# A delta-rule and Mish kernel on one core: sign by Prelu, one join for two, low bits on GpSimd, and a new work order

## The chip, the cores and the metric

The kernel runs on one core of one Trainium2 chip. The metric is the device time of one execution in microseconds (us); lower is better. The core has five instruction queues that are spoken of here: TensorE (PE in the profile; PEld is its weight load), VectorE (DVE), ScalarE (ACT), GpSimd (POOL) and SyncE (SP, which here only issues transfers). Each queue is carried out in the order in which it is written: an instruction that waits holds up everything behind it on its engine.

## What is computed

Two parts, the second fed by the first. A delta rule runs over 768 steps for 32 heads of 48 dimensions, and a feed-forward layer takes its output:

```python
k_n = k / (norm(k) + 1e-06)
for t in range(S):
    y[t] = q[t] @ state
    state = state + beta[t] * outer(k_n[t], v[t] - k_n[t] @ state)
x = y.transpose(0, 2, 1, 3).reshape(3072, 384)
h = x @ w_in
g = h * tanh(softplus(h))
out = g @ w_out
```

q, k, v and beta arrive as fp32. w_in (384 x 2048) and w_out (2048 x 384) arrive as fp64, and the core has to turn them into pairs of 32-bit numbers (a high part and what is left) before the layer can use them.

## The kernel before

**The delta rule.** Time is cut into 12 chunks n of 64 steps, taken in pairs g = n // 2. For a pair, `early` turns k round (L546), forms the products of the keys with each other on TensorE (`gram`), takes the norms' square roots (`norms`, `guess`, `root`) and solves a triangular system on VectorE, step by step (L688 and L689, two instructions a step). For g = 0 and 1 the system is solved in halves of 16, which `merge` joins with two sets of small products, `ma` and `mb`, and an addition on VectorE (L748). Then, for each chunk, TensorE's products `ta`, `tb` (stages `s_a2` and `s_b2`), `gq`, `pz` and `py`/`ps` (`s_gq`, `s_z`, `s_y`) give the chunk's output y and carry the state on; ScalarE and VectorE copy every result out of PSUM before the next product can use it.

**The layer.** `moe(n)` works on the 256 rows of one chunk: 8 times `up` (L1122, 18 products each, tile `h`), Mish on ScalarE (L1139, tile `e`), a high and a low part of the result (L1140 on ScalarE, L1141 on VectorE, tile `g`), and `down` (L1133, 12 products each, tile `acc`).

**The weights.** `convert(k)` turns one of 28 pieces of fp64 words (`parts`: 12 of w_in, tiles `ri`, 512 columns; 16 of w_out, tiles `ro`, 384 columns; four `o` behind every three `i`) into two fp32r tiles. The steps are: ScalarE scales the upper words by 2^-112 (L437); GpSimd clamps (L451) and writes sign times zero over the upper words (L448), VectorE doing the clamp of piece 6; VectorE joins twice (L455: once shifted left by 3 with the sign, once with the lower words shifted right by 29); ScalarE writes the high part (L467); the low part is a subtraction on VectorE (L478) for pieces 0 to 10, and for pieces 11 to 27 two products on TensorE (L472, L474) that ScalarE copies out (L476). `cvd` says which piece an `up` or a `down` needs: `up` 0 and 1 need pieces 0 to 2, `up` 2 and 3 pieces 7 to 9, and so on.

**The order.** No instruction is placed by hand. Every piece of work is an `op` with an engine, an estimated duration, a rank (`prio`), its predecessors and its buffers; `Plan.run` plays the program through with these estimates, always takes the ready piece of best rank, and so writes each engine's queue. It also estimates the transfers (`kb`, `line`, `flying`), and where it sees TensorE idle during the first part it puts in products on zeros (`fill`, L527, and `tiny`, L512), which keep TensorE busy and compute nothing. Its estimates set the order alone; on the chip every engine waits on semaphores for what it really needs. Transfers of weights go to SP in order; from piece 6 on, the load of piece k is issued only after L437 of piece k - 4 (`PACE`).

Of the kernel before, what the change touches and what calls it, by code (L numbers as in the profile page):

```python
# [10 lines left out]
I32 = mybir.dt.int32  # L11
BF16 = mybir.dt.bfloat16
# [56 lines left out]
class Plan:  # L69
# [48 lines left out]
    def run(self):  # L118
        there, due, group, cold = self.THERE, None, False, True
        free, line, used, ready, flying, chain = {}, 0.0, self.used, {}, [], {}  # L120
        for o in self.ops:
# [3 lines left out]
            free.setdefault(o.engine, 0.0)  # L125
# [9 lines left out]
        def when(o):  # L135
            late = 0.0 if o.engine != "PE" else 0.12 if o.prio < -50 else 0.12 + (self.MARGIN if o.prio < 1.9 else 0.1)
            t = max([a.free + (late if not a.kb or o.prio < -50 or o.prio > 1.5 else 2.5) if a.engine != o.engine or (a.kb and o.sync) else a.start + a.took
# [12 lines left out]
            if o.kb and len(flying) >= 8:  # L150
                t = max(t, flying[-8])
# [6 lines left out]
        while todo:  # L158
# [32 lines left out]
            if o.words and self.FILL_FROM < t < self.FILL_TO:  # L191
                us = self.SHARE * (t - free[e]) - 0.2
                n = self.fill(us) if us > self.FILL else 0
                if n:
                    _, there, due = self.feed(free[e], us, 4 * n, there, due, line)
            free[e] = t + o.took
            if o.words:
                _, there, due = self.feed(t, o.took, o.words, there, due, line)
            if o.kb:

                line = max(line, t + 1.6)
                line += o.kb
                o.free = line + 0.8
                flying.append(o.free)
            else:
                o.free = t + o.took + self.SEEN[e]
# [22 lines left out]
def kernel(  # L229
# [16 lines left out]
    P = 128  # L246
# [165 lines left out]
    def convert(k, got, loads):  # L412
# [23 lines left out]
        def scaled():  # L436
            marks[copied[k]] = nc.scalar.activation(a(), words()[:, :, 1].bitcast(F32), AF.Copy, scale=2.0 ** -112).ins  # L437
# [22 lines left out]
        e = "DVE" if k in SIGN_DVE else "POOL"  # L460
        o = op(e, 0.13 + 0.38 * u if e == "DVE" else 0.3 + 0.45 * u, prio, lambda: sign(e), o, bufs=held)
        o = op("DVE", 0.05 + 0.65 * u, prio, lambda: join(words()[:, :, 1], 3, ALU.logical_shift_left), o, bufs=held)
        o = op("DVE", 0.05 + 0.65 * u, prio, lambda: join(words()[:, :, 0], 29, ALU.logical_shift_right), o, bufs=held)
# [6 lines left out]
        if k in LO_PE:  # L470
# [3 lines left out]
            p2 = op("PE", 0.03 + 0.22 * u, prio, lambda: nc.tensor.matmul(  # L474
# [62 lines left out]
    def early(g, at, gate=None):  # L537
# [102 lines left out]

        def root():

            ss, y, rc, nb = (small[x] for x in ("ss", "y", "rc", "nb"))
# [3 lines left out]
            nc.vector.reciprocal(rc, ss)  # L647
            nc.vector.scalar_tensor_tensor(nb, rc, -1.0, rc, op0=ALU.mult, op1=ALU.mult)
# [8 lines left out]
        def scale():  # L657
            nb = small["nb"]
            nc.vector.tensor_tensor(out=nb, in0=nb, in1=betaT[:, g, :], op=ALU.mult)
# [643 lines left out]
```

## Time and profile before

| | us |
| --- | --- |
| median of 3 runs | 616.37 |
| lowest, highest run | 615.85, 617.23 |
| the profiled execution's own time | 618.65 |
| its span, first to last instruction | 616.9 |
| PE busy in the span | 595.7 (97%) |
| DVE busy | 433.4 (70%) |
| ACT busy | 269.3 (44%) |
| POOL busy | 161.5 (26%) |

The table is read from the top of the profile's page. The 40 slices of the page show TensorE at nine tenths or more from the seventh slice on, and gaps and a lower granted clock in the slices before; VectorE is busiest in the first third. The work of the first third is therefore looked at in order of time, and the rest only as a sum.

### The profile page before, as it was taken

How to read it: one execution, taken by the hardware profiler on the slowest of the kernel's cores; microseconds unless marked ns; L12 is line 12 of the kernel's file. 1: busy time of each engine (PE TensorE's matmuls, PEld its weight loads, DVE VectorE, ACT ScalarE, POOL GpSimd, SP SyncE). 2: the span in 40 equal slices, each digit the busy share in tenths (PEclk: the TensorE clock that was granted, in tenths of full speed). 3: DMA queues.
4: the chain of work that ended last, by engine and by line, in shares of the span. 5: the costliest groups of instructions: out<-in, count | busy, mean ns of one | idle time of the engine just before them, and what ended most of it. 6: DMA issues, size and time to landing. Idle time of an engine off the chain costs nothing.

```text
span 616.9 us, 23665 instructions
## 1 busy us (share of the span) xinstructions
PE 595.7 (97%) x10358; PEld 546.6 (89%) x10358; DVE 433.4 (70%) x947; ACT 269.3 (44%) x577; POOL 161.5 (26%) x321
## 2 busy tenths in 40 slices
PE   8859989999999999999999999999999999999997
PEld 4536868898999999999999999999999999999996
DVE  4847999797169988489998399987698983741110
ACT  2824769742444323544333634334534236353231
POOL 6519945243001350212241113502013501000000
PEclk9986899999999999999999999999999999999999
DMA  7885775421015222234214053223032230110011
GB/s 119 206 178 154 214 181 120 66 41 29 3 25 84 41 41 39 41 44 84 46 20 72 4 87 58 42 27 54 16 66 41 40 52 3 23 34 1 2 27 26
DMA packets 158408, 37.80 MB, mean 61 GB/s; under 512 B 151649, under 2 KB 154721, under 8 KB 158305
## 3 DMA queue, kind: packets, MB, share of 16 engines
q1 hardware_dynamic: 153632, 35.85, 30.1%
q8 instruction: 81, 1.33, 0.9%
q10 hardware_dynamic: 4672, 0.44, 0.6%
q14 instruction: 23, 0.18, 0.1%
HBM read 31.56 MB, written 4.72 MB: 59 GB/s over the span
## 4 chain that ended last, share of the span: by engine, by line
PE 87%; DVE 4%; DMA 3%; SPq 2%; issue 2%; ACT 1%; ACTq 0%; DVEq 0%
PE acc L1133 34%; PE h L1122 33%; PE py L766 4%; PE gq L766 3%; PE pz L766 2%; PE pg L562 2%; PE tb L766 2%; PE ps L766 2%; SPq L347 1%; DMA qsrc<-in_q_dram 1%; PE acc L527 1%; PE ta L766 1%; DMA ri<-in_moe_w_in_dram 1%; DMA ksrc<-in_k_dram 1%; PE loo L472 1%
## 5 line engine op out<-in xcount | busy, mean ns | idle before, releaser
L1122 PE MATMUL h<-x,wi 128*128 128x256 f32 x1728 | 221.5, 284 | 0.9 <-ACT e L1139 0.9
L1133 PE MATMUL acc<-wo,g 128*128 128x384 f32 x1152 | 220.8, 342 | 0.3 <-issue 0.3
L1122 PEld LDWEIGHTS h<-x,wi 128*128 128x128 f32 x1728 | 213.7, 189 | 3.4 <-ACT e L1139 1.0
L1133 PEld LDWEIGHTS acc<-wo,g 128*128 128x128 f32 x1152 | 199.7, 188 | 4.0 <-issue 0.7
L1141 DVE TENSOR_TENSOR g<-e,g 128x512 fp32r<-128x512 f32 x96 | 68.3, 716 | 104.1 <-ACT g L1140 103.8
L1139 ACT ACTIVATE e<-h 128x512 f32<-128x512 f32 x96 | 57.4, 598 | 121.4 <-PE h L1122 84.2
L1140 ACT CAST g<-e 128x512 fp32r<-128x512 f32 x96 | 59.4, 619 | 102.3 <-PE acc L1133 101.4
L925 POOL TENSOR_SCALAR vt<-vt,ne 128x48 f32<-128x48 f32 x176 | 74.4, 448 | 61.2 <-DMA vt<-in_v_dram 36.5
L689 DVE TENSOR_TENSOR gt<-gt,pr 128x84 f32<-128x84 f32 (+14 forms) x148 | 47.7, 322 | 5.1
L688 DVE TENSOR_TENSOR pr<-gt 128x84 f32<-128x84 f32 (+14 forms) x148 | 47.3, 319 | 3.3
L719 POOL COPY tt<-tt 32x512 f32<-32x512 f32 x24 | 16.4, 685 | 118.4 <-DVE tt L702 85.3
L591 POOL TENSOR_SCALAR_AFFINE_SELECT d<-at 32x512 f32<-32x512 f32 x20 | 16.5, 826 | 86.0 <-ACT at L582 85.3
L983 DVE TENSOR_TENSOR xx<-gq,amask 64x256 f32<-64x256 f32 x88 | 37.1, 422 | 1.7
L976 DVE TENSOR_TENSOR vt<-vt,gq 64x192 f32<-64x192 f32 (+1 forms) x66 | 23.3, 353 | 20.2 <-PE gq L766 19.5
L790 ACT COPY xx<-pz 64x192 f32<-64x192 f32 x92 | 28.9, 314 | 15.5 <-PE pz L766 14.2
L934 DVE STREAM_TRANSPOSE xx<-qsrc 64x512 f32<-64x512 f32 x44 | 31.1, 706 | 1.3
L766 PE MATMUL gq<-xx,kt 64*64 64x112 f32 (+1 forms) x768 | 29.4, 260 | 0.7 <-DVE tt L748 0.7
L1080 DVE TENSOR_TENSOR xx<-xx,ps 48x192 f32<-48x192 f32 x80 | 28.2, 352 | 2.6 <-PE ps L766 0.9
L766 PEld LDWEIGHTS py<-xx 128*32 128x32 f32 (+1 forms) x1536 | 22.2, 106 | 5.5 <-issue 4.3
L766 PE MATMUL pz<-vt,tt 64*64 64x48 f32 x768 | 26.8, 225 | 0.0
L766 PEld LDWEIGHTS pz<-vt,tt 64*64 64x64 f32 x768 | 22.0, 140 | 5.3 <-ACT tt L790 1.3
L527 PE MATMUL warm<-zcol,identr 128*128 128x421 f32 (+10 forms) x62 | 26.6, 564 | 0.0
(149 smaller groups left out, 595.1 us busy)
## 6 DMA issues: line engine op xcount, KB each, us to landing
ri<-in_moe_w_in_dram SPq DMA_DIRECT2D x12, 512.0 KB, 5.4
ro<-in_moe_w_out_dram SPq DMA_DIRECT2D x16, 384.0 KB, 4.7
vt<-in_v_dram SPq DMA_DIRECT2D x24, 192.0 KB, 4.2
xx<-in_k_dram SPq DMA_DIRECT2D x48, 96.0 KB, 3.0
out_dram<-o SPq DMA_DIRECT2D x48, 96.0 KB, 2.2
ksrc<-in_k_dram SPq DMA_DIRECT2D x44, 64.0 KB, 2.7
qsrc<-in_q_dram SPq DMA_DIRECT2D x44, 64.0 KB, 2.6
ksrc<-in_k_dram SPq DMA_DIRECT2D x44, 32.0 KB, 3.0
```

What stands on the lines that cost most here:

```text
L527: nc.tensor.matmul(to()[:, 512 - w:], ident, zcol.broadcast_to([P, w]), start=free, stop=free)
L688: nc.vector.tensor_tensor(out=pv, in0=nj, in1=xj, op=ALU.mult)
L689: return nc.vector.tensor_tensor(out=below, in0=below, in1=pv, op=ALU.add).ins
L766: last = nc.tensor.matmul(*a, **flags)
L925: nc.gpsimd.tensor_scalar(vt()[:, p, :], vt()[:, p, :], ne()[:, n16 + p:n16 + p + 1], 1.0, op0=ALU.mult, op1=ALU.mult)
L934: nc.vector.transpose(xx[h][r, :, hh, Q0:K0], src)
L983: nc.vector.tensor_tensor(out=x[r, p4, hh, Q0:K0], in0=pg[h4]()[i, :, d:], in1=bcast_mid(amask[i], 4), op=ALU.mult)
L1122: nc.tensor.matmul(h()[:, f2, :], wt["i", f * P // WI * NCH + c][:, i2, f0:f0 + P], x[:, c, :], start=(i == 0), stop=(i == 3 * NCH - 1))
L1133: nc.tensor.matmul(acc[t]()[:, :DM], gg()[:, a, f2, ts_], wt["o", f][:, i2, :], start=(f == 0 and i == 0), stop=(f == NF - 1 and i == 2))
L1139: m = op("ACT", 0.58, prio + 0.1, lambda e=e, h=h: nc.scalar.activation(e(), h(), AF.Mish, scale=-1.0), m, bufs=[h, e])
L1140: m = op("ACT", 0.58, prio + 0.1, lambda e=e, gg=gg: nc.scalar.copy(out=gg()[:, 0], in_=e()), m, bufs=[e, gg])
L1141: m = op("DVE", 0.72, prio + 0.1 - PRIO_XT * (n == 1), lambda e=e, gg=gg: nc.vector.tensor_tensor(out=gg()[:, 1], in0=e(), in1=gg()[:, 0], ...
```

## The change

**Conversion.** L437's copy becomes a Prelu with scale 2^-112 and slope 2^32 for negative numbers (L453 in the new file). A negative number so comes out with an exponent whose bits, shifted left by 3, leave the sign bit set; the lower clamp's bound is scaled to match. The sign's instruction on GpSimd goes. In its place GpSimd turns the lower words into their top three bits (L464: times 2^-29, at most 7, read as unsigned and written as integers), which needs only the loaded piece and not the scaled one. One join on VectorE (L471) takes the place of two.

**First chain.** `root` is split. `least` and `square` form the reciprocal of the squared norm for the system straight from the root (one reciprocal in place of two before `scale`); what gives the norms themselves (`ne`) becomes an op of its own that can stand later, and `bp` is written by ScalarE. `ta` no longer waits for `tn`. The first `up` waits for the two high parts of y alone, and `up` does the products with the low part of x last.

**Account and ranks.** The estimate of transfers is new (`LINE`, `RING`, `HELD_UP`), and all ranks and constants are new. Low parts on TensorE begin at piece 13 in place of 11; no weight is loaded before q and v (`EW` = 0 in place of 1).

```diff
-            marks[copied[k]] = nc.scalar.activation(a(), words()[:, :, 1].bitcast(F32), AF.Copy, scale=2.0 ** -112).ins
+            marks[copied[k]] = nc.scalar.activation(a(), words()[:, :, 1].bitcast(F32), AF.Prelu, scale=2.0 ** -112, alpha=2.0 ** 32).ins
...
-        def sign(engine):
-            s = words()[:, :, 1].bitcast(F32)
+        def low(engine):
+            x = words()[:, :, 0]
             if engine == "DVE":
-                nc.vector.tensor_scalar(words()[:, :, 1], words()[:, :, 1], -2 ** 31, None, op0=ALU.bitwise_and)
+                nc.vector.tensor_scalar(x, x, 29, None, op0=ALU.logical_shift_right)
             else:
-                nc.gpsimd.tensor_scalar(s, a(), 0.0, 1.0, op0=ALU.mult, op1=ALU.mult)
+                nc.gpsimd.tensor_scalar(x, x.bitcast(U32), 2.0 ** -29, 7.0, op0=ALU.mult, op1=ALU.min)
...
-            engine.tensor_scalar(a(), a(), F64_MOST * 2.0 ** -112, -F64_MOST * 2.0 ** -112, op0=ALU.min, op1=ALU.max)
+            engine.tensor_scalar(a(), a(), F64_MOST * 2.0 ** -112, -F64_MOST * 2.0 ** -80, op0=ALU.min, op1=ALU.max)
...
-        o = op("DVE", 0.05 + 0.65 * u, prio, lambda: join(words()[:, :, 1], 3, ALU.logical_shift_left), o, bufs=held)
-        o = op("DVE", 0.05 + 0.65 * u, prio, lambda: join(words()[:, :, 0], 29, ALU.logical_shift_right), o, bufs=held)
+        t = op(e, 0.13 + 0.38 * u if e == "DVE" else 0.3 + 0.45 * u, prio + LOWER, lambda: low(e), got)
+        o = op("DVE", 0.05 + 0.65 * u, prio, join, o, t, bufs=held)
...
+        def square():
+            s1, y, rc, nb = (small[x] for x in ("s1", "y", "rc", "nb"))
+            nc.vector.scalar_tensor_tensor(s1, y, 4e-6, s1, op0=ALU.mult, op1=ALU.add)
+            nc.vector.reciprocal(rc, s1)
+            nc.vector.scalar_tensor_tensor(nb, rc, -1.0, betaT[:, g, :], op0=ALU.mult, op1=ALU.mult)
...
-            m = op("PE", 2.14, prio, up, *xdn[n], *(cvd["i", 2 * fp * P // WI * NCH + c] for c in range(NCH)),
+            m = op("PE", 2.14, prio, up, *xdn[n][::1 if n or fp else 2], *(cvd["i", 2 * fp * P // WI * NCH + c] for c in range(NCH)),
...
-    VACT, LOP, FIRST = 1, 11, 0
-    BURN1, BURN2, BURN3, BURN4, BURN5 = 0, 0, 0, 16, 0
+    VACT, LOP, FIRST, ROOT, LATE_BY = 1, 13, 0, 0.536, 10
+    BURN1, BURN2, BURN3, BURN4, BURN5 = 0, 0, 0, 0, 16
...
-    KW, EW, BURN, TQ, PACE = 1, 1, 116, 1, 4
+    KW, EW, BURN, TQ, PACE = 3, 0, 84, 1, 4
```

**Where the order moves, first place.** VectorE's queue from the end of the first solve (the transposition into `tt_82`) to the addition that follows `mb`; `mi` and `spare` are pieces being converted, `ri`/`ro` their words, and `spare_750` and `spare_791` are both piece 6. Before:

```order
L702 STREAM_TRANSPOSE tt_82<-gt_319 128x32x32
L455 SCALAR_TENSOR_TENSOR mi_345<-mi_345,ri_230 128x512
L455 SCALAR_TENSOR_TENSOR mi_345<-ri_230,mi_345 128x512
L455 SCALAR_TENSOR_TENSOR mi_416<-mi_416,ri_313 128x512
L478 SCALAR_TENSOR_TENSOR wi_745<-mi_345,wi_745 128x512
L455 SCALAR_TENSOR_TENSOR mi_416<-ri_313,mi_416 128x512
L451 TENSOR_SCALAR spare_750<-spare_750 128x384
L478 SCALAR_TENSOR_TENSOR wi_758<-mi_416,wi_758 128x512
L748 TENSOR_TENSOR tt_82<-tt_82,mb_765 128x16x16
L751 STREAM_TRANSPOSE tn_838<-tt_82 128x512
```

The same stretch in the changed kernel:

```order
L726 STREAM_TRANSPOSE tt_82<-gt_315 128x32x32
L471 SCALAR_TENSOR_TENSOR mi_444<-mi_444,ri_313 128x512
L471 SCALAR_TENSOR_TENSOR mi_458<-mi_458,ri_318 128x512
L493 SCALAR_TENSOR_TENSOR wi_698<-mi_444,wi_698 128x512
L493 SCALAR_TENSOR_TENSOR wi_704<-mi_458,wi_704 128x512
L471 SCALAR_TENSOR_TENSOR mi_609<-mi_609,ri_320 128x512
L772 TENSOR_TENSOR tt_82<-tt_82,mb_720 128x16x16
L775 STREAM_TRANSPOSE tn_794<-tt_82 128x512
L493 SCALAR_TENSOR_TENSOR wi_788<-mi_609,wi_788 128x512
L893 TENSOR_SCALAR at_219<-ta_799 32x8x32 x2
L467 TENSOR_SCALAR spare_791<-spare_791 128x384
```

The clamp of piece 6 has moved from two places ahead of the addition to four places behind it.

**Second place.** ScalarE's queue around the first two Mish of the layer (tiles `e_0` and `e_1`). Before:

```order
L1082 COPY xx_81<-ps_11_1146 48x4x48 x2
L467 ACTIVATE wi_1202<-solved 128x512
L1139 ACTIVATE e_0_1271<-h_0_1085 128x512
L437 ACTIVATE spare_831<-ro_874 128x384
L437 ACTIVATE solved<-ri_1072 128x512
L467 ACTIVATE wo_1282<-mo_1060 128x384
L736 ACTIVATE ym_232<-ma_1205 128x16x16
L437 ACTIVATE solved<-ri_1104 128x512
L1139 ACTIVATE e_1_1312<-h_1_1163 128x512
L437 ACTIVATE mi_1319<-ri_1142 128x512
```

In the changed kernel:

```order
L1106 COPY xx_81<-ps_11_1142 48x4x48 x2
L1160 ACT_TABLE_LOAD
L1160 ACTIVATE e_0_1190<-h_0_1103 128x512
L453 ACT_TABLE_LOAD
L453 ACTIVATE solved<-ri_1073 128x512
L1160 ACT_TABLE_LOAD
L1160 ACTIVATE e_1_1215<-h_1_1161 128x512
L482 ACTIVATE wo_1288<-spare_827 128x384
L453 ACT_TABLE_LOAD
L453 ACTIVATE mi_1293<-ri_1086 128x512
```

Prelu and Mish are not in the same table of functions, so a load of the table stands between them wherever they follow each other. The kernel before has 4 such loads in all, the changed one 14: one of the ten new ones ahead of the first Prelu, nine from `e_0` to `e_4`, while the conversion goes on. The estimates in `Plan` do not hold them.

## Rows read from the trace of the kernel before

**Rows 1.** The page: shares of the chain that ended last, by engine.
```profile
PE 87%; DVE 4%; DMA 3%; SPq 2%; issue 2%; ACT 1%; ACTq 0%; DVEq 0%
```

**Rows 2.** Busy us (xcount) of PE, PEld, DVE, ACT, POOL by stretch; PEclk, DMA share, GB/s.
```profile
44.00:57.60 13.60, 11.74 (x154) 8.36 (x154) 9.50 (x18) 5.76 (x13) 11.78 (x20) 0.53 0.57 195
...
60.40:124.40 64.00, 60.66 (x1034) 49.85 (x1036) 57.77 (x95) 48.13 (x105) 36.19 (x50) 0.97 0.61 141
...
156.70:616.90 460.20, 455.49 (x7706) 436.26 (x7704) 312.52 (x707) 185.22 (x395) 79.34 (x166) 1.00 0.23 38
```

**Rows 3.** Timeline of DVE: start, us, instruction, [idle before <- who ended it].
```profile
15.81 0.35 DVE L644 RECIPROCAL rc<-y 128x32 f32<-128x32 f32 x1 [0.30 <-ACT y L628]
...
17.44 0.19 DVE L659 TENSOR_TENSOR nb<-nb,betaT 128x32 f32<-128x32 f32 x1 [0.21 <-DMA qsrc<-in_q_dram]
...
18.62 0.16 DVE L688 TENSOR_TENSOR pr<-gt 128x28 f32<-128x28 f32 x1
...
21.54 0.70 DVE L688 TENSOR_TENSOR pr<-gt 128x108 f32<-128x108 f32 x1
...
24.61 0.27 DVE L688 TENSOR_TENSOR pr<-gt 128x108 f32<-128x108 f32 x1
...
30.33 1.96 DVE L702 STREAM_TRANSPOSE tt<-gt 128x1024 f32<-128x1024 f32 x1
...
43.18 0.36 DVE L451 TENSOR_SCALAR spare<-spare 128x384 f32<-128x384 f32 x1 [7.53 <-ACT spare L437]
...
44.30 0.41 DVE L748 TENSOR_TENSOR tt<-tt,mb 128x256 f32<-128x256 f32 x1
```

**Rows 4.** Timeline of ACT: the wait for piece 6.
```profile
42.60 0.54 ACT L437 ACTIVATE spare<-ro 128x384 f32<-128x384 f32 x1 [8.28 <-DMA ro<-in_moe_w_out_dram]
```

**Rows 5.** Timeline of PE; a filler on zeros is warm or acc from zcol.
```profile
31.85 4.08 PE L527 MATMUL warm<-zcol,identr 128*128 128x453 f32 x10
35.86 1.26 PE L743 MATMUL mb<-tt,ym 32*32 32x16 f32 x128
...
44.77 1.97 PE L766 MATMUL ta<-tt,at 32*64 32x64 f32 x32 [6.30 <-DVE tt L748]
...
50.06 2.36 PE L766 MATMUL tb<-at,tn 32*64 32x64 f32 x32 [1.09 <-ACT at L867]
...
61.56 2.62 PE L1122 MATMUL h<-x,wi 128*128 128x256 f32 x18
...
84.59 1.15 PE L766 MATMUL ta<-tt,at 32*64 32x64 f32 x32
...
123.80 1.10 PE L766 MATMUL py<-xx 128*32 128x64 f32 x64
...
125.34 4.50 PE L1133 MATMUL acc<-wo,g 128*128 128x384 f32 x24
129.68 6.64 PE L1122 MATMUL h<-x,wi 128*128 128x256 f32 x54
...
143.54 1.83 PE L527 MATMUL acc<-zcol,identr 128*128 128x128 f32 x14
```

**Rows 6.** Timeline of POOL during the first solve.
```profile
21.48 0.67 POOL L448 TENSOR_SCALAR ri<-mi 128x512 f32<-128x512 f32 x1
```

**Rows 7.** Groups by line and shape: line engine op out<-in xcount | busy us, mean ns.
```profile
L455 DVE SCALAR_TENSOR_TENSOR mi<-mi,ri 128x512 int32<-128x512 int32 x6 | 4.9, 816 | 0.0
...
L476 ACT ACTIVATE wo<-loo 128x384 fp32r<-128x384 f32 x11 | 5.3, 487 | 1.8 <-PE loo L474 1.5
...
L467 ACT ACTIVATE wo<-spare 128x384 fp32r<-128x384 f32 x7 | 3.6, 521 | 2.3 <-DVE spare L455 2.2
```

**Rows 8.** Timeline of ACT around a table load of the second pair.
```profile
127.82 0.62 ACT L1140 CAST g<-e 128x512 fp32r<-128x512 f32 x1 [2.37 <-PE acc L1133]
128.46 1.28 ACT L627 ACT_TABLE_LOAD   x1
129.75 0.23 ACT L628 ACTIVATE y<-ss 128x32 f32<-128x32 f32 x1
```

More of the change, by code (lines that the diff above doesn't have):

```diff
@@ L105, in feed @@
                 done = t + self.TAKES + min(2.6, max(0.0, line - t))
+                line = max(line, t) + self.BEHIND
             if left <= 0:
-                return t, there, done
+                return t, there, done, line
             n = min(left, there)
@@ L119, in run @@
         there, due, group, cold = self.THERE, None, False, True
-        free, line, used, ready, flying, chain = {}, 0.0, self.used, {}, [], {}
+        free, line, used, ready, ring, chain, issued = {}, 0.0, self.used, {}, [], {}, 0
         for o in self.ops:
@@ L124, in run @@
                 a.next.append(o)
-            free.setdefault(o.engine, 0.0)
+            free.setdefault(o.engine, self.BEGIN)
             ready.setdefault(o.engine, [])
@@ L136, in when @@
             late = 0.0 if o.engine != "PE" else 0.12 if o.prio < -50 else 0.12 + (self.MARGIN if o.prio < 1.9 else 0.1)
-            t = max([a.free + (late if not a.kb or o.prio < -50 or o.prio > 1.5 else 2.5) if a.engine != o.engine or (a.kb and o.sync) else a.start + a.took
+            t = max([a.free + (late if not a.kb or o.prio < -50 or o.prio > 1.5 else self.LATER) if a.engine != o.engine or (a.kb and o.sync) else a.start + a.took
                      for a in o.after], default=0.0)
@@ L194, in run @@
                 if n:
-                    _, there, due = self.feed(free[e], us, 4 * n, there, due, line)
+                    _, there, due, line = self.feed(free[e], us, 4 * n, there, due, line)
             free[e] = t + o.took
             if o.words:
-                _, there, due = self.feed(t, o.took, o.words, there, due, line)
+                _, there, due, line = self.feed(t, o.took, o.words, there, due, line)
             if o.kb:
[L201 to L204, printed above, removed]
+                us, rows = self.LINE[o.kb]
+                begin = max(line, t + self.LEAD)
+                line = begin + us
+                o.free = line + self.LANDS
+                ring.append((begin, line, rows))
+                most = self.RING
+                for x0, x1, n in reversed(ring[-30:]):
+                    if n > most:
+                        o.took = max(o.took, x0 + (x1 - x0) * (n - most) / n - t)
+                        break
+                    most -= n
+                if e == "SP":
+                    o.took += self.HELD_UP.get(issued, 0.0)
+                    issued += 1
+                if us < 0.05:
+                    o.took += 0.35
+                free[e] = t + o.took
             else:
@@ L657, in scale, with opposite @@
         def scale():
[L658 to L659 removed]
             nc.vector.tensor_tensor(out=grid(), in0=grid(), op=ALU.mult,
[L661 to L665 removed]
+                                    in1=small["nb"].rearrange("p (x j) -> p x j", x=nb_).unsqueeze(2).broadcast_to(by_col))
+        def opposite():
+            nc.scalar.mul(out=bp(), in_=small["nb"], mul=-1.0)
+        known = betas if g == 0 else ()
         if g < ROOTS:
             o = op("DVE", 0.38, at(0.25), norms, o, last_s.get("root"), bufs=[gr])
+            l = op("DVE", 0.16, at(0.25), least, o)
             o = op("ACT", 2.7 if g else 1.4, at(0.25), guess, o)
             last_s.setdefault("guess", o)
[L671 removed]
+            y = o = op("DVE", 0.82, at(0.25), square, o, l, *known)
         else:
[L673 to L674 removed]
+            y = o = op("DVE", 3.3, at(0.25), lambda: (norms(), least(), steps(), square()), o, last_s.get("root"), *known, bufs=[gr])
+        bp_ = op("ACT", 0.24, at(0.26), opposite, o, last_s.get("turned"), bufs=[bp])
+        o = op("DVE", 0.71 if split else 1.23, at(0.26), scale, o, cut, bufs=[gr])
         nes[g] = ne
[L676 removed]
+        ned[g] = last_s["root"] = op("DVE", 1.05, at(ROOT), root, y, last_s.get("turned"), bufs=[ne])
         e = "DVE" if split else "POOL"
```

61 lines of the change are left out of this document (27 added, 34 removed).

## The prediction

> **What bounds the kernel now.** The page's chain comes first: 87% of it is TensorE [rows 1]. The second view is the table of stretches. From 156.70 us on TensorE is busy 455.5 of 460.2 us at a granted clock of 1.00 [rows 2]. The change removes no work there except by order, so the rest of the span moves as a block, and what counts is when TensorE has done the work of the first 130 us. Two stretches decide that.
>
> The first runs to the first `up` at 61.56 [rows 5]. TensorE stands idle for 6.30 us before `ta`, waiting for VectorE's addition L748. The addition was ready early, since `mb` had ended at 37.1; but it stood behind the clamp of piece 6, on which VectorE waited 7.53 us [rows 3], because ScalarE had waited 8.28 us for the transfer of that piece [rows 4]. After that the granted clock is 0.53 of full speed [rows 2], and `ta` and `tb` take 1.97 and 2.36 us, where `ta` later takes 1.15 [rows 5].
>
> The second is the conversion, from 60.4 (the second high part of y is written) to 124.4 (the last low part is copied). In those 64.0 us VectorE is busy 57.8, ScalarE 48.1 and GpSimd 36.2 [rows 2]. TensorE's 60.7 hold waiting that the view counts as busy, since ends are modelled. VectorE is the fullest of the three that feed it. At 129.68 the first `up` of the next chunk starts [rows 5]; I use it as the mark.
>
> **The first solve.** From the root's arrival to the first step VectorE needed 15.81 to 18.62, with a wait for q's transfer ending at 17.44 [rows 3]. Three instructions (0.35, 0.19, 0.19) now replace five, q is loaded ahead of any weight, and `bp` and `ne` leave: I take 1.2 less. `root`'s second half returns within the steps with four instructions: 1.05 more. GpSimd now does seven conversion instructions during the solve in place of four. What one costs VectorE is seen in a pair of equal size: the product of 108 columns takes 0.70 while L448 runs on GpSimd and 0.27 without [rows 3, 6]: three more by 0.43, 1.3 more. Bounds are nothing, and 0.67 each, GpSimd's whole instruction. The Trainium skill (SBUF — State Buffer, "SBUF: two separate sides") says that the pair of ports is locked for a whole instruction; by it the three would cost 2.0. So `tt` ends at 32.3 - 1.2 + 1.05 + 1.3 = 33.4.
>
> **The addition.** VectorE then has three joins and two low parts ahead of it, about 0.75 each (0.82 for a join, under contention [rows 7]): 37.2. TensorE's side agrees: `ma` starts 1.15 after the transposition (about 31.5), takes 1.2, then six filler passes of 487 columns come in place of ten of 453, which took 4.08 [rows 5]: 2.6, then `mb` 1.26, which gives 36.6. So the addition starts at 37.2 and not at 44.30: **7.1 earlier**. What is late next is ScalarE's Prelu of piece 6, which still stands ahead of `at`'s copies; its load should be issued near 30 where it was issued at 38, so I cost it at nothing; if its cover fails, the wait is at most the old 8.28 [rows 4].
>
> **To the first `up`.** From the addition to `ta` 0.47, as before; `ta` 1.15; about 1.1 to `tb`; `tb` 1.2; 2.1 to `pz` (two joins stand ahead of VectorE's copy); `pz` 1.3: 44.5. The clock fell to its low level, 1.2 GHz, at the end of the idle 6.30 us; without that gap I take the high one, 2.4 GHz, throughout. Then fillers: ten passes of 412 columns, 3.7; two `py` and half of `ps`, 2.6 [rows 5]; eight passes, 3.0. The first `up` starts at 53.8 (**7.8 earlier**), and the second high part of y is written at about 51, where it was 60.4.
>
> **The conversion, by ScalarE.** VectorE loses one join of 0.6 to 0.8 for each piece [rows 7], some 11 us of its 57.8 in this stretch. GpSimd keeps two instructions a piece; I cost its new one as the old one, 0.67 for 512 columns [rows 6]. ScalarE becomes the fullest. By count of the order it does, in the same stretch, four high parts, one copy-or-Prelu, two low parts, two Mish and one cast less: 4 x 0.52 + 0.55 + 2 x 0.49 + 2 x 0.60 + 0.62 = 5.4 [rows 4, 7, 8]. Prelu I cost as the copy it replaces, 0.54 for 384 columns [rows 4]. Nine table loads come in. A load took 1.28; it started 0.02 after the cast before it had ended, and the next instruction started 0.01 after the load [rows 8]. So 48.1 - 5.4 + 9 x 1.28 = 54.2 without a wait. Before, ScalarE waited 15.9 of the 64.0, mostly on a fuller VectorE; I take a third, 5, with 0 and 15.9 as the ends. The last low part is then copied at 51 + 54.2 + 5 = 110.2 and not at 124.4.
>
> The Trainium skill (ScalarE: Activation LUTs, "What ACT_TABLE_LOAD costs") gives 1.28 for the load, which the row agrees with, and 1.38 more for emptying the engine, which no row here shows; the nine would cost 24.0 by it, and its rule to batch by set speaks against this change.
>
> **The mark.** TensorE's last product for a low part ended at 123.9, half a microsecond ahead of that copy [rows 5], so now at 109.7; then it had 5.8 us left to 129.68. Now it has two `up` (2 x 2.2), `py` with `ps` (1.54) and two `down` (2 x 2.17): 10.3 [rows 5], and one `down` more is still owed: 109.7 + 10.3 + 2.2 = 122.2, **7.5 earlier**. Behind the mark, the second pair's solve waits for a buffer that the last pieces hold, so it moves with them. At the `ma` there 16 fillers (32 passes at 0.126, 4.0) are written; before, 14 passes stood ahead of it [rows 5], more behind, with waiting. I take 1 less, between 1 more and 3 less. Sum: **8.5 less**. The later order, the split `up`, `bp` on ScalarE and the dropped waits for `tn` I cost at nothing, covered by TensorE's queue; if the cover goes, 1 us either way. The profiled execution, 618.65, would become 610.2; the median, 2.3 below it, 607.9.
>
> **Rivals.** (1) *ScalarE waits as long as before on top of its loads.* The loads sit between a Mish and a Prelu that each wait for another engine, and the order was written without them. With 15.9 of waiting the last copy is at 121.1, the mark's work 3.4 late, the kernel 2.4 slower: **618.8**. It decides from 13.5 us of waiting. For it: PE, POOL and ScalarE form a ring. Against: VectorE, which made it wait, is relieved. (2) *A switch empties the engine.* Each load would then wait out what is in it, bounded by rows at one instruction, 0.62 [rows 8]: 9 x 0.62 = 5.6, **613.5**. Row 128.46 speaks against it. By the 1.38 that the Trainium skill gives (the section above) it would be 620.3. (3) *ScalarE hardly waits*, and the fillers are well cut: 5 more at the conversion, 1.5 more in all else, about **601.4**. (4) *GpSimd's unsigned read costs double*: five such stand ahead of the first clamp, 5 x 0.67 = 3.3 later: **611.2**. (5) *Transfers hold the pace*, and the pieces need 64 us as before: last copy at 115, 4.8 more: **612.7**; the DMA share of 0.61 [rows 2] speaks against it. That the joins give the wanted bits is a matter of the output and moves no time.
>
> **How the numbers follow.** Forecast (605 to 610.5) 0.50, (3) 0.18, (1) 0.10, (4) 0.10, (5) 0.08, (2) 0.04. The range, 601 to 616, reaches from (3) over (2), (4) and (5), and leaves out (1) and a better case than (3). A measurement here can tell about 0.2%, 1.2 us. Faster takes the forecast, (3) and most of (4) and (5): 0.82; within 0.2%, from (1), (4) and (5): 0.06; slower, most of (1) and half of (2): 0.12.
>
> **What would show it.** Right: VectorE's addition near 37 with no wait for piece 6, the first `up` at 52 to 55, 14 table loads of 1.28 with ScalarE over 85% busy in the conversion, the next chunk's first `up` at 117 to 123. Wrong: ScalarE idle 12 us or more there, L464 over 1 us each, or a new wait for a transfer ahead of `ta`.

## The result and the profile after

The changed kernel takes 620.94 us (median of 4 runs, 620.44 to 621.4) where the kernel before took 616.11 beside it: a ratio of 1.008, 95% interval 1.006 to 1.010, **slower by 4.8 us**. The prediction was 607.9 with a range of 601 to 616 and faster at 0.82. It is wrong in sign and outside its range. The profiled execution of after took 621.4 us, its span is 619.7.

The first view is the page's chain, shares by engine, of the changed kernel; it answers to [rows 1].

```profile
PE 84%; POOL 4%; DVE 4%; ACT 3%; DMA 2%; issue 2%; SPq 0%; ACTq 0%; POOLq 0%; DVEq 0%
```

GpSimd, which had no part in the chain before, now has 4%. The groups by line and shape on GpSimd from 20 to 124 us show why (line, engine, operation, tile, shapes, count, busy us, mean ns, idle before):

```profile
L464 POOL TENSOR_SCALAR ro<-ro 128x384 int32<-128x384 uint32 x16 | 28.1, 1755 | 1.3
L464 POOL TENSOR_SCALAR ri<-ri 128x512 int32<-128x512 uint32 x12 | 25.0, 2087 | 1.9 <-DMA ri<-in_moe_w_in_dram 1.0
...
L467 POOL TENSOR_SCALAR mi<-mi 128x512 f32<-128x512 f32 x6 | 4.1, 685 | 0.5 <-ACT mi L453 0.2
```

The new instruction takes 2.09 us for 512 columns, where the clamp of the same size takes 0.69 and the old sign instruction took 0.67 [rows 6]. The 28 of them hold GpSimd for 53.1 us. The windows of after, same columns and the same first two stretches as [rows 2], show what that does:

```profile
44.00:57.60 13.60, 12.73 (x256) 8.40 (x257) 11.08 (x20) 8.35 (x20) 12.87 (x14) 0.71 0.64 146
60.40:124.40 64.00, 55.16 (x909) 43.69 (x910) 35.66 (x60) 50.32 (x95) 48.21 (x49) 0.92 0.56 123
```

In the 64 us of the old conversion VectorE is busy 35.7 where it was 57.8; GpSimd went from 36.2 to 48.2, and is busy 56.4 of the 60 us from 40 to 100. VectorE's timeline says for whom it waits (start, us, instruction, [idle before <- who ended it]):

```profile
64.65 0.85 DVE L471 SCALAR_TENSOR_TENSOR mo<-mo,ro 128x384 int32<-128x384 int32 x1 [3.59 <-POOL mo L467]
...
73.33 0.95 DVE L471 SCALAR_TENSOR_TENSOR spare<-spare,ro 128x384 int32<-128x384 int32 x1 [4.52 <-POOL spare L467]
```

The releaser named is the clamp L467, a cheap instruction; what makes it late is the L464 that stand ahead of it in GpSimd's queue. GpSimd's timeline up to these two clamps:

```profile
60.85 3.18 POOL L464 TENSOR_SCALAR ro<-ro 128x384 int32<-128x384 uint32 x2
64.11 0.51 POOL L467 TENSOR_SCALAR mo<-mo 128x384 f32<-128x384 f32 x1
...
70.71 1.99 POOL L464 TENSOR_SCALAR ri<-ri 128x512 int32<-128x512 uint32 x1
72.79 0.51 POOL L467 TENSOR_SCALAR spare<-spare 128x384 f32<-128x384 f32 x1
```

From 20 to 124 us VectorE's join L471 waits 18.9 us in all for L467. ScalarE hands the wait on, and TensorE gets it:

```profile
65.59 0.52 ACT L482 ACTIVATE wo<-mo 128x384 fp32r<-128x384 f32 x1 [4.94 <-DVE mo L471]
...
68.34 1.28 ACT L1160 ACT_TABLE_LOAD   x1
69.63 0.60 ACT L1160 ACTIVATE e<-h 128x512 f32<-128x512 f32 x1
70.25 1.28 ACT L453 ACT_TABLE_LOAD   x1
71.54 0.67 ACT L453 ACTIVATE solved<-ri 128x512 f32<-128x512 f32 x1
```

```profile
38.11 1.78 PE L790 MATMUL ta<-tt,at 32*64 32x64 f32 x32
...
49.50 4.97 PE L542 MATMUL warm<-zcol,identr 128*128 128x412 f32 x10
...
59.40 0.72 PE L1144 MATMUL h<-x,wi 128*128 128x256 f32 x2
...
70.28 2.08 PE L1144 MATMUL h<-x,wi 128*128 128x256 f32 x8 [4.62 <-ACT e L1160]
...
132.71 2.31 PE L1144 MATMUL h<-x,wi 128*128 128x256 f32 x18
```

The wait of 3.59 on VectorE at 64.65 becomes 4.94 on ScalarE at 65.59, which stands in front of the first Mish, and that Mish ends the 4.62 us of idle TensorE ahead of 70.28. The solve did get faster: `ta` starts at 38.11, where it started at 44.77 [rows 5]. But the granted clock was low from 38.4 to 52.0, so `ta` and ten fillers took 1.78 and 4.97, and the first `up` came at 59.40, 2.2 earlier than before and not 7.8. The mark, the first `up` of the next chunk, is at 132.71 against 129.68 [rows 5], with one `down` more still owed.

Three theories were left by this trace. **A**: GpSimd's integer instruction is the bound. **B**: the ten table loads in the conversion are. **C**: the new order of the start and its low clock cost the time.

### The profile page after: what moved, and what is told of

It reads as the page before. It is cut to its first block, busy times and chain, and to the rows that moved or that the text cites. A ratio compares the mean times of both kernels' runs of the same rounds, so it can differ in the third digit from the quotient of the medians.

```text
span 619.7 us, 23624 instructions
## 1 busy us (share of the span) xinstructions
PE 598.8 (97%) x10336; PEld 548.2 (88%) x10336; DVE 416.0 (67%) x921; ACT 282.2 (46%) x591; POOL 191.4 (31%) x321
## 4 chain that ended last, share of the span: by engine, by line
PE 84%; POOL 4%; DVE 4%; ACT 3%; DMA 2%; issue 2%; SPq 0%; ACTq 0%; POOLq 0%; DVEq 0%
PE acc L1154 33%; PE h L1144 32%; PE py L790 4%; PE gq L790 3%; PE pz L790 2%; PE ps L790 2%; POOL ri L464 2%; PE pg L577 2%; PE tb L790 1%; PE ta L790 1%; PE acc L542 1%; POOL ro L464 1%; PE warm L542 1%; DMA qsrc<-in_q_dram 1%; DMA ksrc<-in_k_dram 1%
## 5 line engine op out<-in xcount | busy, mean ns | idle before, releaser
L1144 PE MATMUL h<-x,wi 128*128 128x256 f32 x1728 | 224.9, 286 | 5.1 <-ACT e L1160 4.6
L1144 PEld LDWEIGHTS h<-x,wi 128*128 128x128 f32 x1728 | 216.6, 192 | 8.3 <-ACT e L1160 4.8
L1154 PE MATMUL acc<-wo,g 128*128 128x384 f32 x1152 | 218.6, 338 | 0.0
L1154 PEld LDWEIGHTS acc<-wo,g 128*128 128x128 f32 x1152 | 196.7, 188 | 3.2
L1162 DVE TENSOR_TENSOR g<-e,g 128x512 fp32r<-128x512 f32 x96 | 66.6, 695 | 109.3 <-ACT g L1161 109.1
L949 POOL TENSOR_SCALAR vt<-vt,ne 128x48 f32<-128x48 f32 x176 | 72.8, 438 | 97.6 <-DVE ne L672 83.2
L713 DVE TENSOR_TENSOR gt<-gt,pr 128x84 f32<-128x84 f32 (+14 forms) x148 | 47.2, 319 | 5.1
L606 POOL TENSOR_SCALAR_AFFINE_SELECT d<-at 32x512 f32<-32x512 f32 x20 | 14.5, 725 | 95.2 <-ACT at L597 47.4
L542 PE MATMUL warm<-zcol,identr 128*128 128x412 f32 (+10 forms) x70 | 29.6, 563 | 0.0
L464 POOL TENSOR_SCALAR ro<-ro 128x384 int32<-128x384 uint32 x16 | 28.1, 1755 | 1.3
```

The costliest lines, as they stand in the source:

```text
L464: nc.gpsimd.tensor_scalar(x, x.bitcast(U32), 2.0 ** -29, 7.0, op0=ALU.mult, op1=ALU.min)
L542: nc.tensor.matmul(to()[:, 512 - w:], ident, zcol.broadcast_to([P, w]), start=free, stop=free)
L713: return nc.vector.tensor_tensor(out=below, in0=below, in1=pv, op=ALU.add).ins
L949: nc.gpsimd.tensor_scalar(vt()[:, p, :], vt()[:, p, :], ne()[:, n16 + p:n16 + p + 1], 1.0, op0=ALU.mult, op1=ALU.mult)
L1144: nc.tensor.matmul(h()[:, f2, :], wt["i", f * P // WI * NCH + c][:, i2, f0:f0 + P], x[:, c, :], start=(i == 0), stop=(i == 3 * NCH - 1))
L1154: nc.tensor.matmul(acc[t]()[:, :DM], gg()[:, a, f2, ts_], wt["o", f][:, i2, :], start=(f == 0 and i == 0), stop=(f == NF - 1 and i == 2))
```

## The experiments

A ratio is to the kernel before, in runs on the same chip, with its 95% interval. A difference between two medians can be some 1 us off where they were taken apart: the median of the kernel before was 616.00 to 616.99 beside the different runs. Where nothing else is said, a kernel is the changed one with the diff shown. Where a mark is given, five `down` are done by it, as in after, and in e6 six.

### GpSimd's instruction in float32 (e1)

```diff
-                nc.gpsimd.tensor_scalar(x, x.bitcast(U32), 2.0 ** -29, 7.0, op0=ALU.mult, op1=ALU.min)
+                nc.gpsimd.tensor_scalar(x.bitcast(F32), words()[:, :, 1].bitcast(F32), 0.0, 1.0, op0=ALU.mult, op1=ALU.mult)
```

> The changed kernel, every engine's order unchanged; GpSimd's 28 instructions on the low words have the same places and 8-byte strides, but read and write float32 (the high word times zero, the form of the old sign instruction) in place of uint32 to int32. The lowest three bits of each weight are left out. Theory A (the integer form of this instruction, 1.75 us for 384 columns and 2.0 to 2.1 us for 512, makes GpSimd the bound of the conversion): an instruction falls to 0.60 and 0.67 us, 16 x 1.15 + 12 x 1.4 = 35 us of GpSimd's time go, VectorE's waits of 1.5 to 4.5 us on it go, and the time falls to 606 to 613 us. Theory B (the ten table loads of 1.28 us between Prelu and Mish hold ScalarE): 617 to 621 us, since the loads stay. Theory C (the new order of the start with its half clock at 38 to 52 us): 617 to 621 us as well.

Measured: 612.95 us, ratio 0.994 (0.991 to 0.996), that is 8.0 below the changed kernel. No engine's order changed. The groups of GpSimd, the windows and TensorE's timeline of this kernel:

```profile
L464 POOL TENSOR_SCALAR ro<-ro 128x384 f32<-128x384 f32 x16 | 11.1, 703 | 3.1 <-DMA ro<-in_moe_w_out_dram 2.7
...
L464 POOL TENSOR_SCALAR ri<-ri 128x512 f32<-128x512 f32 x12 | 9.9, 827 | 3.7 <-DMA ri<-in_moe_w_in_dram 3.1
```

```profile
44.00:57.60 13.60, 13.52 (x310) 9.85 (x311) 12.34 (x22) 10.89 (x25) 10.96 (x17) 1.00 0.98 208
60.40:124.40 64.00, 57.91 (x999) 47.73 (x1000) 41.42 (x80) 54.97 (x102) 28.01 (x45) 0.95 0.60 122
```

```profile
37.58 1.15 PE L790 MATMUL ta<-tt,at 32*64 32x64 f32 x32
...
45.59 3.74 PE L542 MATMUL warm<-zcol,identr 128*128 128x412 f32 x10
...
54.26 2.62 PE L1144 MATMUL h<-x,wi 128*128 128x256 f32 x18
...
122.61 2.31 PE L1144 MATMUL h<-x,wi 128*128 128x256 f32 x18
```

The trace of this run is the prediction's kernel with about its assumed price: the first `up` is at 54.26 (forecast 53.8), the last low part is copied by 112.9 (forecast 110.2), the mark is at 122.6 (forecast 120.0, and 122.2 with the `down` still owed), and the profiled execution took 610.55 (forecast 610.2). The median, 612.95, is further off (forecast 607.9). 32 us of GpSimd's time and 10.1 us at the mark hang on the form of one instruction; VectorE's waits for L467 from 20 to 124 us fall from 18.9 to 10.1. Of the 10.1 us at the mark 5.1 are there at the first `up`. TensorE's idle time ahead of the third `up` is not the loss: e1 has 4.06 us there as well, only 6.5 us earlier. Theory A holds; C in its plain form falls, since the order is the same, and the clock is 1.00 from 30 to 60 us.

### Copy in place of Prelu (e2), and both (e3)

```diff
-... AF.Prelu, scale=2.0 ** -112, alpha=2.0 ** 32).ins
+... AF.Copy, scale=2.0 ** -112).ins
```

> The changed kernel, with Copy in place of Prelu in ScalarE's first pass: same reads and writes, same order, but ten table loads of 1.28 us fewer. The signs of the weights are left out, GpSimd's instructions stay as they are. Theory A (GpSimd is the bound): ScalarE only waits longer, 618.5 to 621.5 us. Theory B (the loads): most of 12.8 us comes back, 608 to 613 us. Theory C (order and clock of the start): 618 to 621 us.

Measured: 617.45 us, ratio 1.002 (1.001 to 1.003), 3.5 below the changed kernel. The mark is at 129.5. Ten loads, 12.8 us of ScalarE, give back 3.5: neither theory's number. GpSimd takes most of the room, but the loads are not free behind it.

> Both edits: float32 low words as in the first run and Copy in place of Prelu as in the second; the lowest three bits and the signs of the weights are left out. Theory A: with GpSimd out of the way ScalarE is the next bound, so the loads now count in part: 1 to 5 us below the first run, 603 to 610 us. Theory B: as the second run within 1 us, 608 to 613 us. Theory C: 615 to 620 us, since neither touches the start.

Measured: 606.21 us, ratio 0.983 (0.981 to 0.986). One sentence of the expectation needs a correction: the signs are not left out here, because the high word times zero keeps its sign and the join sets it; what is left out is the lowest three bits. The mark is at 118.55. The two edits alone give 8.0 and 3.5, together 14.7; at the mark 10.1 and 3.2, together 14.2. So each hides part of the other, by the medians more than by the mark. The windows, as before:

```profile
60.40:124.40 64.00, 60.60 (x1032) 50.94 (x1032) 48.64 (x94) 45.57 (x96) 33.04 (x62) 0.97 0.64 129
```

With GpSimd at 33.0, ScalarE at 45.6 and VectorE at 48.6 no engine but TensorE is near full. So A is the first limit and B the second, 6.7 us by the medians and 4.1 at the mark once the first is gone.

### Where the price bites (e9)

```diff
+                if k < 7:
+                    nc.gpsimd.tensor_scalar(x.bitcast(F32), words()[:, :, 1].bitcast(F32), 0.0, 1.0, op0=ALU.mult, op1=ALU.mult)
+                else:
                     nc.gpsimd.tensor_scalar(x, x.bitcast(U32), 2.0 ** -29, 7.0, op0=ALU.mult, op1=ALU.min)
```

> The changed kernel, same order; only the first seven pieces have the float32 form on GpSimd (their lowest three bits are left out), the other 21 keep the integer one. It tells where the price bites. If it is paid ahead of the first clamps, as the prediction's fourth rival had it, the first up product comes back from 59.4 to about 54.3 us, where the run with all 28 in float32 had it, and the time falls by the most of 8.0 us, to 613 to 615 us. If it is paid all through the conversion, the first up comes back but the later pieces still wait for GpSimd: 616 to 619 us.

Measured: 619.02 us, ratio 1.003 (1.001 to 1.005), 1.9 below the changed kernel. TensorE's timeline:

```profile
55.25 2.62 PE L1147 MATMUL h<-x,wi 128*128 128x256 f32 x18
...
130.73 2.31 PE L1147 MATMUL h<-x,wi 128*128 128x256 f32 x18
```

The first `up` comes back by 4.2 us, and the granted clock of 40 to 60 us is 1.00 again; at the mark only 2.0 of the 4.2 are left. The later 21 pieces wait for GpSimd whatever the start has won: it is busy 56.5 of the 60 us from 40 to 100, as in after. The price is one of throughput, paid all through the conversion.

### What in the instruction costs (e5)

```diff
-                nc.gpsimd.tensor_scalar(x, x.bitcast(U32), 2.0 ** -29, 7.0, op0=ALU.mult, op1=ALU.min)
+                z = words()[:, :, 1].bitcast(F32)
+                h_ = raw[kind, i].bitcast(mybir.dt.uint16).rearrange("p (a b) -> p a b", b=4)[:, :, 1]
+                b_ = raw[kind, i].bitcast(mybir.dt.uint8).rearrange("p (a b) -> p a b", b=8)[:, :, 3]
+                o, i_, m_ = ((x, x.bitcast(U32), 2.0 ** -29), (x, z, 0.0), (x.bitcast(F32), x.bitcast(U32), 0.0),
+                             (x, x, 0.0), (x, h_, 2.0 ** -13), (x, b_, 2.0 ** -5))[k % 6]
+                nc.gpsimd.tensor_scalar(o, i_, m_, 7.0, op0=ALU.mult, op1=ALU.min)
```

> A measurement of the disputed cost by itself: the changed kernel, same order, with GpSimd's instruction on the low words in six forms that take turns from piece to piece: uint32 to int32 (the change's own), float32 to int32, uint32 to float32, int32 to int32, uint16 to int32, uint8 to int32, all multiply and then minimum, all over words 8 bytes apart. All but the first lack correct low bits. Theory A says that the price is in the integer conversion: if reading costs, the two forms with float32 on that side take 0.6 to 0.9 us and the others about 1.7 for 384 columns; if writing costs, uint32 to float32 is the cheap one; if every pass through integers costs, each has half of the extra 1.15 us. A rival: the price is the 32-bit width of the read, then uint16 and uint8 are cheap. No time is compared.

Measured (620.07 us in one run), GpSimd's groups by shape and type:

```profile
L469 POOL TENSOR_SCALAR ro<-ro 128x384 int32<-128x384 uint32 x4 | 6.5, 1618 | 0.3
L469 POOL TENSOR_SCALAR ri<-ri 128x512 f32<-128x512 uint32 x3 | 6.3, 2115 | 0.2
L469 POOL TENSOR_SCALAR ri<-ri 128x512 int32<-128x512 int32 x3 | 6.1, 2049 | 0.2
L469 POOL TENSOR_SCALAR ro<-ro 128x384 int32<-128x384 uint8 x3 | 5.6, 1852 | 0.2
L469 POOL TENSOR_SCALAR ro<-ro 128x384 int32<-128x384 f32 x3 | 5.1, 1708 | 0.2
L469 POOL TENSOR_SCALAR ri<-ri 128x512 int32<-128x512 uint16 x2 | 4.5, 2242 | 0.2
L469 POOL TENSOR_SCALAR ri<-ri 128x512 int32<-128x512 f32 x2 | 4.0, 1991 | 0.2
L469 POOL TENSOR_SCALAR ro<-ro 128x384 f32<-128x384 uint32 x2 | 3.8, 1916 | 0.2
...
L469 POOL TENSOR_SCALAR ro<-ro 128x384 int32<-128x384 uint16 x2 | 3.1, 1534 | 0.2
```

None of the expected pictures is right. An integer on either side costs the whole price: 512 columns take 1.99 with only the output an integer, 2.12 with only the input, 2.05 with both, and a narrow read saves little or nothing (2.24 for uint16, and 1.53 for 384 columns of it, where uint32 took 1.62). With float32 on both sides they took 0.83 in e1. That form multiplies twice where these take a minimum; the minimum isn't the price, since the float32 clamp L467, a minimum and a maximum, takes 0.69. So there is no cheap integer form of this instruction among these; the work must go to another engine or stay in float32.

### The old conversion in the new plan (e6), the new one in the old plan (e7)

In e6 the functions `scaled`, `sign`, `clamp` and `join` of the kernel before stand in the changed kernel; in e7 those of the changed kernel stand in the kernel before. The planner lays both out anew.

> The changed kernel with the conversion of the kernel before (Copy, GpSimd's float32 sign, two joins by VectorE); everything else of the change (transfer account, first chain, ranks) stays and the planner lays it out anew. Nothing is left out. Theory A: the start keeps its gain and the conversion its old pace, 606 to 613 us, less than before. Theory C (the new start and ranks are worth nothing or cost time): 616 to 622 us.

> The kernel before with the changed conversion alone (Prelu, GpSimd's integer low words, one join), planned by the old account and ranks. Nothing is left out. Theory A: GpSimd gets 28 x about 1.2 us more and was at 0.9 of its time from 50 to 70 us, so the conversion ends later: 620 to 630 us. Theory C (the conversion is no loss, the new start is): 612 to 617 us.

Measured: e6 617.05 us, ratio 1.002 (1.000 to 1.003); e7 634.5 us, ratio 1.031 (1.028 to 1.035), with its mark at 148.05. e6 falls out as theory C had it, e7 beyond A's range. Both agree that the new conversion is the loss (with the new plan it costs 3.9 us, with the old one 18), but e6 also says that the new start is worth nothing with the old conversion. Its trace shows a gain first: the first `up` is at 52.2, the mark at 124.80, 4.9 earlier than before and with as many `down` done. Of that gain 2.9 go afterwards: behind the mark e6 needs 490.1 us and the kernel before 487.2. The other 2.0 stand between the two profiled executions alone (616.59 and 618.65) and not between the medians. TensorE's timeline of e6 ahead of the second solve:

```profile
130.21 7.19 PE L543 MATMUL acc<-zcol,identr 128*128 128x128 f32 x62
137.33 1.26 PE L756 MATMUL ma<-tu,d 16*32 16x16 f32 x128
```

The plan puts 62 passes on zeros, 7.19 us, in front of `ma`, where the kernel before had 14 in 1.83 [rows 5]; and from 240 to 600 TensorE is idle for 1.3 us where it was idle for 0.01. So part of the time won in the first 125 us is spent as filler ahead of `ma`; how the rest of the 2.9 comes about in an order laid out anew isn't shown.

### The planner told the true cost (e8)

```diff
-        t = op(e, 0.13 + 0.38 * u if e == "DVE" else 0.3 + 0.45 * u, prio + LOWER, lambda: low(e), got)
+        t = op(e, 0.13 + 0.38 * u if e == "DVE" else 0.6 + 1.5 * u, prio + LOWER, lambda: low(e), got)
```

> The changed kernel with one number of its planner altered: the low words on GpSimd cost 0.6 + 1.5 us per 512 columns in its account instead of 0.3 + 0.45, so the order is laid out with the cost that the trace shows. Nothing is left out. If the loss is only an order planned on a wrong cost, 608 to 614 us. Theory A in its strict form (GpSimd lacks the time whatever the order): 617 to 622 us.

Measured: 635.67 us, ratio 1.032 (1.030 to 1.033), slower by far than expected of either. The first `up` is at 67.7 and the mark at 139.6. GpSimd's queue shows a reason: its first clamp L467 starts at 55.15, behind 14 of the L464, where it started at 30.32 behind five in after. An order planned on the true cost, with the ranks left as they are, doesn't save the change. That no order could isn't shown: the ranks were not set again.

### The low words on VectorE (e4), and fewer low parts on TensorE (e10)

```diff
-    LOW_DVE = []
+    LOW_DVE = list(range(len(parts)))
```

> The changed kernel with the low words on VectorE instead of GpSimd, for all 28 pieces, by its branch with the integer shift; nothing is left out, and the planner lays the order out anew. Theory A: GpSimd is left with the clamps alone (28 x 0.65 us); VectorE carries 28 x about 0.5 us = 14 us more, 72 of the 64 us between 60 and 124 if nothing else moved, so it is tight: 608 to 615 us. Theory B: 618 to 622 us, the loads stay. Theory C: the start is planned anew, so 612 to 622 us.

Measured: 612.28 us, ratio 0.993 (0.991 to 0.996), as A expected. The change as it is, with its own branch for VectorE, is faster than the kernel before. The integer shift costs little there:

```profile
L462 DVE TENSOR_SCALAR ro<-ro 128x384 int32<-128x384 int32 x16 | 7.0, 459 | 0.3 <-DMA ro<-in_moe_w_out_dram 0.2
L462 DVE TENSOR_SCALAR ri<-ri 128x512 int32<-128x512 int32 x12 | 6.2, 533 | 0.0
```

13.2 us on VectorE replace 53.1 on GpSimd. In e10, LOP goes from 13 to 20 on top of that.

> The run with the low words on VectorE, and the low parts of pieces 13 to 19 made by VectorE instead of TensorE and ScalarE as well (one number; the planner lays the order out anew; nothing is left out). If ScalarE with its ten loads is the bound that is left there, seven copies of about 0.5 us leave it and 2 to 4 us come back: 608 to 611 us. If VectorE is the bound already, 612 to 617 us.

Measured: 618.3 us, ratio 1.003 (1.001 to 1.005), 6 above e4. The reason given for that outcome is not what the trace shows: VectorE isn't full (47.2 of 64 us from 56 to 120), and the mark is at 122.79, 2.8 *earlier* than e4's 125.54 with as many `down` done. What is lost is lost behind it, as part of the gain is in e6. The matmuls on zeros, in the groups from 125 to 600 us, of e4 and of e10:

```profile
L542 PE MATMUL acc<-zcol,identr 128*128 128x128 f32 x52 | 6.7, 275 | 0.0
```

```profile
L542 PE MATMUL acc<-zcol,identr 128*128 128x128 f32 x102 | 12.9, 277 | 0.0
```

6.2 us more of them, and 1.3 of idle time from 240 on against 0.3, is 7.2. The loss to account for is 6.4: 3.6 between the spans of the profiled executions, and the 2.8 won at the mark. Whether the passes make the delay or fill one was the last question (e12), with `FILL_TO` set from 200 to 120 in e10:

> The run with the low parts of pieces 13 to 19 on VectorE (618.3 us), and the planner writes no matmuls on zeros behind its time 120 (FILL_TO from 200 to 120); the order of the rest is laid out anew, much as it was. Nothing is left out. That run was 2.8 us ahead at the mark of the run with the low words on VectorE and lost 6.4 behind it, with 50 more passes on zeros, 6.2 us. If the passes themselves cost the time, 612 to 615 us. If they fill a wait of TensorE for the second solve's first operand that is there anyway, 617 to 620 us with idle time in their place, or more where the clock falls in it.

Measured: 616.64 us, ratio 1.001 (0.999 to 1.003), 1.7 below e10. TensorE's timeline of e12:

```profile
142.39 1.25 PE L755 MATMUL ma<-tu,d 16*32 16x16 f32 x128 [3.75 <-DVE tu L724]
```

Idle time stands in place of the filler ahead of `ma`: TensorE waits for VectorE's `tu` and goes on 0.14 after its end. VectorE begins the second solve (`ss`) at 125.50 in e10 and at 123.11 in e4, 2.4 later, though TensorE is 2.8 earlier at the mark. But that is not where e10 falls behind e4. Its `ma` starts at 144.66 where e4's starts at 144.39, and the third chunk's `pz` starts at 171.0 where e4's starts at 172.2. The lead is lost between there and the third chunk's first `up`. TensorE's timeline of e10, and then the same `up` in e4:

```profile
175.76 2.36 PE L1154 MATMUL acc<-wo,g 128*128 128x384 f32 x12
178.05 1.10 PE L790 MATMUL py<-xx 128*32 128x64 f32 x64
...
185.07 2.05 PE L542 MATMUL acc<-zcol,identr 128*128 128x128 f32 x16
...
188.65 2.27 PE L542 MATMUL acc<-zcol,identr 128*128 128x128 f32 x18
...
193.52 6.72 PE L1144 MATMUL h<-x,wi 128*128 128x256 f32 x54
```

```profile
191.11 8.79 PE L1144 MATMUL h<-x,wi 128*128 128x256 f32 x72
```

In e10 two `down` stand in front of this `py`, which starts 7.0 after `pz`, against 3.7 in e4. The layer's work is then used up, and 44 passes on zeros, 5.7 us, stand where e4 has four. So, by the trace, the 2.8 won in the conversion goes as filler in an order that puts the second chunk's layer ahead of the third chunk's chain; an order that keeps this chain ahead was not tried. The passes are not free either: in e10 `ma` starts 2.2 after the end of its `tu`, behind them, and in e12, without them, the third chunk's first `up` is 5.5 earlier. Of this, 2.8 are left between the spans of the profiled executions and 1.7 between the medians, whose intervals overlap.

### Half and half (e11)

```diff
+        if k < NEW_TO:
...
+        else:
...
-    LOW_DVE = []
-    LOWER = -4.258
+    LOW_DVE = list(range(len(parts)))
+    LOWER, NEW_TO, SIGN_DVE = -4.258, 14, []
```

The branch below 14 holds the changed conversion, the other one that of the kernel before.

> The first 14 pieces, all scaled ahead of the first Mish, with Prelu and the low words on VectorE; the other 14 with the conversion of the kernel before (Copy, GpSimd's float32 sign, two joins). Nothing is left out; the planner lays the order out anew. Eight of the ten table loads in the conversion go, and VectorE gets 14 x about 0.25 us more than with all pieces on the new way. Theory A with the loads as the second bound: 605 to 610 us, faster than both kernels. If VectorE becomes the bound again, as before the change: 612 to 617 us.

Measured: 607.02 us (604.73 to 610.5), ratio 0.985 (0.981 to 0.990), **faster than both kernels** with nothing left out. The windows and the mark:

```profile
60.40:124.40 64.00, 59.98 (x906) 49.87 (x904) 59.59 (x111) 45.00 (x94) 32.05 (x53) 0.97 0.59 124
```

```profile
118.81 2.31 PE L1175 MATMUL h<-x,wi 128*128 128x256 f32 x18
```

VectorE is full again, 59.6 of 64.0, yet the mark is 13.9 us earlier than after's. Two loads are left between the first Prelu and the last Mish, at 20.18 and 57.90, where after had ten. The run changes three things against after (where the low words are made, the loads, the way of 14 pieces) and doesn't tell their shares.

## Why the prediction was wrong

**The step that failed** is in "The conversion, by ScalarE": "GpSimd keeps two instructions a piece; I cost its new one as the old one, 0.67 for 512 columns [rows 6]". It measured 2.09, and 1.76 for 384. Both instructions are a multiply and a second operation on as many columns 8 bytes apart; the rows of before held no instruction of GpSimd with an integer operand, so the old one was a bound from below and there was none from above. Rival (4) named the right place, at "double" and "five such stand ahead of the first clamp". Both halves were too small: three times, and 28 pieces (e9). The prediction's own sign of being wrong, "L464 over 1 us each", came true. Against the float32 form of e1 the 28 pieces cost 32 us more (53.1 against 21.0), on an engine that was busy 36.2 of the 64.0 and 11.8 of the 13.6 just before [rows 2]: priced so, GpSimd would have had to stand in the sum beside ScalarE.

**The solve** came out right in its number, the addition at 37.52 against 37.2, and that is luck. VectorE was done earlier than in the sum: `tt` ended at 31.75 and not at 33.4, the joins and low parts at 35.8 and not at 37.2. The 1.3 us more for GpSimd's share did not come: in after four of the five L464 in the solve lengthen one step of VectorE each, by 0.31 to 0.35, though an L464 takes 1.6 to 2.1. The addition then waited for `mb`, whose last part came late; the trace names nothing that held it:

```profile
36.88 0.58 PE L767 MATMUL mb<-tt,ym 32*32 32x16 f32 x48 [1.70 <-issue]
```

```profile
37.52 0.42 DVE L772 TENSOR_TENSOR tt<-tt,mb 128x256 f32<-128x256 f32 x1 [1.72 <-PE mb L767]
```

**To the first `up`** was right in e1 (54.26 against 53.8) and wrong in after (59.40): the sum assumed the high clock throughout, and it was low from 38.4 to 52.0. In e1 and e9, where GpSimd's first seven are cheap, it is 1.00 from 38 to 60. What let it fall isn't settled: after has 1.70 us of idle TensorE in the middle of `mb`, but e3 has 1.55 there, and its clock doesn't fall; and in e4, where GpSimd has none of these instructions, it is low too, from about 42 to 49.

**The conversion and the mark** were nearly right given the price. ScalarE's stretch in e1 is 53.7 us busy and 5.4 idle, forecast 54.2 and 5. It begins 2.7 late, since the second high part of y is written at 53.75 and not at about 51. So the last low part is copied 2.7 later than forecast, and with the `down` still owed the mark stands for 124.8 and not 122.2, so 4.9 earlier than before where 7.5 was forecast. **Behind the mark** the sum took 1 less; e1 has 3.2 less (a span of 608.8 - 124.8 = 484.0 behind it against 616.9 - 129.7 = 487.2). The two errors cancel, and the total of 8.1 agrees with the 8.5 by that luck. How weak the second term is e6 and e10 show: with the order laid out anew 2.9 us (e6) and 6.4 (e10) are lost behind the mark.

The sum took ScalarE as the fullest engine, and e3 bears it out once GpSimd is cheap: without the loads the kernel is 6.7 us faster than e1. The Trainium skill (ScalarE: Activation LUTs, "What ACT_TABLE_LOAD costs") gives 1.28 us for a load and 1.38 for emptying the engine. The rows of after show the first and not the second: the load at 70.25 starts 0.02 after the Mish of 69.63 has ended, and Prelu at 71.54 starts 0.01 after the load. So rival (2) is out. The advice of the Trainium skill on the same page, "Table sets: the hidden batching unit", to batch by set, agrees with e3 against e1, where ten loads fewer are worth the 6.7 us. e11, which has Mish and Prelu apart, is the fastest with nothing left out, but not by that alone.

**The part of the miss that the price doesn't explain.** The forecast of 607.9 is the median of before less the 8.5. The measured median is 13.0 above it: e1 gives back 8.0, and 5.0 stay open. The 8.5 were read off a profiled execution that was 2.3 above its kernel's median, and e1's was its fastest, 2.4 below. So the two traces differ by 8.1 us and the medians by 3.1: with the assumed price the kernel does gain, but in its typical execution 3 us and not 8.5. e1's executions part by their mean granted clock: the three at 0.991 to 0.993 took 610.55 to 611.34 us, the four at 0.985 to 0.987 took 612.95 to 614.7. Which stretch of the others loses the clock isn't on record, so that step of the sum stays open.

**Rival (1)** had the sign right at 618.8, and its condition came true: it asked for 13.5 us of waiting on ScalarE, and after has 13.7 in the 64.0. But ScalarE waited behind GpSimd's dear instruction: from the second high part of y to the last low part it is idle for 12.3 us in after and for 5.4 in e1, in the same order.

## What to carry to other kernels

An elementwise instruction that is moved to another engine, or given other types, has no price until a row shows the same engine with the same types; the row of its float32 neighbour was a lower bound here and nothing more, and an upper bound has to be made up before the sum is trusted. When an engine that was half idle is given work that fills it, the trace names as releaser the cheap instruction behind the dear one: look at what stands ahead of it in its queue. And a gain at an early mark counts only if nothing behind it is planned anew: compare the mark *and* the waits and fillers behind it.

## What the runs showed of the hardware

GpSimd's tensor_scalar over words 8 bytes apart takes 1.53 to 1.92 us for 384 columns and 1.98 to 2.24 for 512 as soon as the input or the output is an integer of any width, and 0.70 and 0.83 with float32 on both sides. The Trainium skill (GPSIMD Engine Reference, "4.1 Engine selection") has one-input elementwise work on GpSimd at roughly line rate, where two-input work is about twice as slow as on VectorE. VectorE's integer shift of the same words takes 0.46 and 0.53 (e4): GpSimd's float32 form takes 1.5 and 1.6 times that, its integer form in after 3.8 and 3.9 times, so the traces don't bear the row out for integers.
